# Order of TensorE products: one idle round moved from round 7 to round 2 in the opened steps of a fused Fourier filter and SiLU network

## The chip, the core and the metric

The kernel runs on one core of a Trainium2 chip. The metric is the device time of one execution in microseconds; the median over several runs is compared. The core has five engines that run their own instruction streams and wait for one another by semaphores: TensorE (PE in the profile, with its weight loads shown apart as PEld), VectorE (DVE), ScalarE (ACT), GpSimd (POOL) and SyncE (SP), which issues most of the transfers.

## What is computed

Two blocks follow each other. The first filters each of 8 sequences of 3008 tokens and 256 channels in the frequency domain; the second is a feed-forward network without a gate, with 2048 inner units.

```python
X = np.fft.rfft(x, axis=1)                  # x: (8, 3008, 256)
Y = X * (filt_r + 1j * filt_i)[None, :, :]
y = np.fft.irfft(Y, n=3008, axis=1)
h = y.reshape(24064, 256) @ w_in            # (256, 2048)
out = (h * (1.0 / (1.0 + np.exp(-h)))) @ w_out
```

All is in float32.

## The kernel before

**Tiles and steps.** The transforms are written as products with small tables of cosines and sines, in stages (`stage1`, `forward`, `inverse`, `stage3`, lines 267 to 588). Their pieces for sequence b + 1 are laid in among the work of the network for sequence b. The network takes a sequence in six pairs of token tiles: two halves, each cut into 256, 256 and 240 columns. For each pair it goes over eight blocks of the inner units. One pair with one block is a step, so there are 48 steps for a sequence (`STEPS`) and 384 in all.

**Two generators for a step.** Both products of the network use a Strassen-like scheme with seven products where eight would be needed. `hidden(step)` (line 719) makes the first layer: products named after their weight block, A11, A12, S2, S1, S3, A22 and S4. It yields between them, so that they stand in rounds 0, 1, 2, 3, 4, 6 and 7 of the step's eight rounds (round 5 has none). `project(step)` (line 778) makes the second layer for the step before, seven products that I call P1 to P7 in the order in which they are issued. Each is added up in one of four PSUM banks over the eight blocks of a pair. A product of 256 columns shows in the trace as two matmuls, each with its weight load.

**What a step waits for.** `hidden` has two PSUM banks, and only one of each. In px, A11, S2, S3 and A22 are added up one on another, and between them ScalarE copies the partial sum away (lines 740, 747 and 753) or applies the silu to it (line 736, after A22). In pyz, one half takes A12 and the other S1 and S4; VectorE combines them with the copies into g (line 703, called from `hidden`): g of round 1 after A12, g of round 4 after S3's copy, g of round 7 after S4. Px and pyz are used again by the next step: its A11 waits until the silu has read px, and its A12 until the last g has read pyz. Two subtractions that finish g of the step before (`finish`, line 767) follow g of round 1 on VectorE; P6 and P7 need them.

**What sets the order.** Every engine works in the order in which the program issues. The loop at line 1141 goes through the rounds of a step. In each round it first lets `hidden` and then `project` go on by one product, and then issues what is planned for that place: evictions, parts of the transform, stores (`put`, `pending`, `until`). In an ordinary step P1 to P7 thus stand in rounds 0 to 6.

**Opened steps.** In 20 of the steps (`opened`, filled by `open_step` at line 658) a transform piece borrows the banks px and pyz before `hidden` takes them. These are, counted within 48 steps, step 4 (six times, `stage1`), step 12 (seven times, `stage3` and `forward`) and step 38 (seven times, `stage3`). There P1 and P2 are issued ahead of the piece, to fill the time until px and pyz are free, and the other five products are held in round 0, so that they begin in round 1. With round 7 also given as held, the five stand in rounds 1 to 5. On VectorE and ScalarE an opened step has, besides the work of every step, the evictions of the piece; step 12 also has two multiplies by the filter (line 468); in step 38 the subtractions of `tokens` (line 709) and, for all sequences but the last, two operations of `fold` (line 394) for a later sequence.

The steps 52, 60 and 86 that are spoken of later are such steps 4, 12 and 38. A name with a prime, as in A11', is the product of the step after.

The loop is this:

```python
if step in opened:
    for _ in range(2):
        next(work[1])                      # P1, P2
until(step - 0.05)                         # the piece
for rnd in range(ROUNDS):
    held = work[1:] if step in opened and rnd in (0, 7) else []
    work = [w for w in work if w in held or next(w, work) is not work]
    until(step + rnd / ROUNDS)
```

Of the kernel before, what the change touches and what calls it, by code (L numbers as in the profile page):

```python
# [167 lines left out]
def kernel(  # L168
# [421 lines left out]
    joined, opened = set(), set()  # L590
# [176 lines left out]
    def finish():  # L767

        for g, n in unfinished:
            combine(v, g[:, 6, 0:n], g[:, 2, 0:n], g[:, 4, 0:n], ALU.subtract)  # L770
            combine(v, g[:, 7, 0:n], g[:, 3, 0:n], g[:, 6, 0:n], ALU.subtract)
        unfinished.clear()
# [5 lines left out]
    def project(step):  # L778

        pair, jp = divmod(step, NJP)  # L780
        n, g = pairs[pair][3], g_t.pop(step)
        if jp == 0:
            acc[pair] = {}
        last = jp == NJP - 1

        order = PROJECT
        if jp == 0 and step in joined:
            order = PROJECT[0:2] + PROJECT[3:5] + PROJECT[2:3] + PROJECT[5:]
        elif jp == 0:
            order = PROJECT[2:3] + PROJECT[0:2] + PROJECT[3:]  # L790
        for c, k, i, h in order:
            if i not in acc[pair]:
                acc[pair][i] = accps.tile([128, 2, 256], FP32, name=f"acc_{pair}_{i}", tag=f"a{i}")

            nc.tensor.matmul(out=acc[pair][i][:, h, 0:n], lhsT=w_t[:, jp, c, 1], rhs=g[:, k, 0:n],  # L795
                             start=(jp == 0 and h == 0), stop=last, skip_group_check=True)
            if last and (h == 1 or i == 3):
                drain(pair, i)
            yield
# [327 lines left out]
    for pair in range(len(pairs)):  # L1127
        step, rnd = combines[pair % per] if pair != 1 else (7, 5)
        pending.append((pair // per * STEPS + step + rnd / ROUNDS, 98, lambda pair=pair: tokens(pair)))
        for chunk in range(2 if pair < len(pairs) - 1 else 0):  # L1130
            step, rnd = stores[pair % per][chunk]
# [4 lines left out]
    def until(time):  # L1136
        while pending and pending[0][0] <= time:
            pending.pop(0)[2]()

    until(-1e-3)  # L1140
    for step in range(n_steps + LAG):
        work = []
        if step < n_steps:
            work.append(hidden(step))
        else:
            finish()
        if step >= LAG:
            work.append(project(step - LAG))
        if step in opened:
            for _ in range(2):  # L1150
                next(work[1])
        until(step - 0.05)
        for rnd in range(ROUNDS):
            held = work[1:] if step in opened and rnd in (0, 7) else []
            work = [w for w in work if w in held or next(w, work) is not work]
            until(step + rnd / ROUNDS)
        assert not work
# [30 lines left out]
```

## Time and profile before

| | before |
|---|---|
| time, median of 3 (lowest, highest) | 2591.37 us (2590.7, 2591.59) |
| span of the profiled execution | 2589.0 us |
| granted TensorE clock, mean | 0.996 |
| instructions | 48366 |
| moved to and from HBM | 96.05 MB read, 81.26 MB written |
| mean HBM traffic over the span | 68 GB/s |

The profile's page gives busy times by engine, the chain of work that ended last (followed back from the last instruction to whatever released each one) and groups of instructions by source line. The timeline gives one line to each run of equal instructions: start and duration in us, engine, line, operation, output <- inputs, and count; in square brackets the idle time of the engine before it, and what ended it. A matmul's end is modelled, so successive matmuls overlap in the timeline; the starts are the ones to go by. The table of waits gives, for each engine and line and what it waited for, the sum in us, the number of times and the longest.

### The profile page before, as it was taken

The page shows a single profiled execution, that of the slowest core. Times are in us where ns is not written, and L with a number is a line of the kernel's source. Part 1 is how long each engine was busy: PE and PEld are TensorE (multiplying, and loading weights), DVE is VectorE, ACT ScalarE, POOL GpSimd, SP SyncE. Part 2 cuts the span into 40 slices and gives each one's busy share as a digit, 9 for nine tenths or more (in the row PEclk, how much of TensorE's full clock was granted, in tenths as well). Part 3 has the DMA queues.
Part 4 walks back from the last instruction along what each step waited for, and adds up shares of the span by engine and source line. Part 5 has one row for each costly group of instructions (what it writes and reads, how often), then busy time and mean ns, then how long its engine had stood idle before and what let it go on. Part 6 is the DMA issues. An engine that isn't in the chain of part 4 may idle for free.

```text
span 2589.0 us, 48366 instructions
## 1 busy us (share of the span) xinstructions
PE 2563.1 (99%) x18972; PEld 2197.7 (85%) x18972; DVE 1681.1 (65%) x3569; ACT 1113.6 (43%) x3014; POOL 424.4 (16%) x672
## 2 busy tenths in 40 slices
PE   8999999999999999999999999999999999999998
PEld 6788888888888888888888888888888888888987
DVE  7766666666666666666666666666666676555554
ACT  3544444444444444444444444444444444444443
POOL 2211211121112111211122111211121112101101
PEclk9899999999999999999999999999999999999999
DMA  8531232222222222231223222331232211210000
GB/s 273 148 86 46 67 84 65 60 57 79 62 63 65 71 64 58 71 77 59 68 54 88 56 66 58 79 73 54 64 73 69 71 47 27 65 20 16 9 17 16
DMA packets 200077, 171.08 MB, mean 66 GB/s; under 512 B 122116, under 2 KB 174196, under 8 KB 199060
## 3 DMA queue, kind: packets, MB, share of 16 engines
q1 hardware_dynamic: 178520, 117.04, 18.9%
q0 software_dynamic: 16928, 44.65, 5.4%
q10 hardware_dynamic: 4400, 6.29, 0.8%
q8 instruction: 149, 2.44, 0.4%
q14 instruction: 80, 0.66, 0.1%
HBM read 96.05 MB, written 81.26 MB: 68 GB/s over the span
## 4 chain that ended last, share of the span: by engine, by line
PE 95%; DMA 2%; ACT 1%; DVE 1%; issue 0%; SPq 0%; ACTq 0%; DVEq 0%
PE acc L795 43%; PE px L732 26%; PE pyz L732 19%; PE pd L560 3%; PE pb L446 2%; PE pc L489 2%; PE pf L416 1%; DMA raw<-in_moe_w_in_dram 1%; DMA w_t<-in_x_dram 0%; DVE g L703 0%; PE pa L342 0%; DMA filt<-in_filt_i_dram 0%; DMA t<-d 0%; DMA e_t<-e_tbl 0%; ACT t L349 0%
## 5 line engine op out<-in xcount | busy, mean ns | idle before, releaser
L795 PE MATMUL acc<-g,w_t 128*128 128x256 f32 (+1 forms) x5376 | 1508.8, 375 | 0.4 <-DVE g L703 0.4
L795 PEld LDWEIGHTS acc<-g,w_t 128*128 128x128 f32 x5376 | 1021.3, 190 | 115.6 <-DVE g L703 0.8
L703 DVE TENSOR_TENSOR g<-pyz,abc 128x256 f32<-128x256 f32 (+1 forms) x1152 | 479.6, 416 | 617.8 <-ACT abc L753 366.5
L703 DVE TENSOR_TENSOR g<-g 128x256 f32<-128x256 f32 (+3 forms) x1152 | 599.1, 520 | 196.9 <-ACT g L736 183.7
L732 PE MATMUL px<-ty,w_t 128*128 128x256 f32 (+1 forms) x2304 | 678.1, 376 | 0.5 <-ACT abc L753 0.5
L736 ACT ACTIVATE g<-g 128x256 f32<-128x256 f32 (+1 forms) x1152 | 472.9, 410 | 242.8 <-DVE g L703 242.8
L732 PEld LDWEIGHTS px<-ty,w_t 128*128 128x128 f32 x2304 | 432.4, 190 | 64.4 <-issue 7.9
L703 POOL TENSOR_TENSOR s<-s 128x256 f32<-128x256 f32 (+1 forms) x329 | 255.0, 793 | 1414.3 <-DVE s L815 1308.9
L732 PE MATMUL pyz<-y,w_t 128*128 128x256 f32 (+1 forms) x1536 | 454.1, 377 | 0.0
L732 PEld LDWEIGHTS pyz<-y,w_t 128*128 128x128 f32 x1536 | 283.4, 189 | 47.4 <-DVE g L703 8.2
L747 ACT COPY abc<-px 128x256 f32<-128x256 f32 (+1 forms) x384 | 141.5, 368 | 367.3 <-PE px L732 367.3
L753 ACT COPY abc<-px 128x256 f32<-128x256 f32 (+1 forms) x384 | 141.9, 369 | 344.7 <-PE px L732 344.7
L736 ACT ACTIVATE g<-px 128x256 f32<-128x256 f32 (+1 forms) x384 | 146.1, 380 | 297.3 <-PE px L732 297.2
L732 PE MATMUL px<-y,w_t 128*128 128x256 f32 (+1 forms) x768 | 234.3, 387 | 2.1 <-ACT y L246 1.0
L732 PE MATMUL pyz<-ty,w_t 128*128 128x256 f32 (+1 forms) x768 | 225.6, 375 | 0.2 <-DVE g L703 0.2
L732 PEld LDWEIGHTS px<-y,w_t 128*128 128x128 f32 x768 | 138.6, 189 | 41.1 <-ACT g L736 7.7
L732 PEld LDWEIGHTS pyz<-ty,w_t 128*128 128x128 f32 x768 | 145.9, 190 | 17.5 <-DVE g L703 1.0
L740 ACT COPY abc<-px 128x256 f32<-128x256 f32 (+1 forms) x384 | 135.8, 354 | 44.6 <-PE px L732 44.6
L560 PEld LDWEIGHTS pd<-wi_t,t 48*64 48x64 f32 x4096 | 68.6, 140 | 30.2 <-ACT g L736 16.4
L560 PE MATMUL pd<-wi_t,t 48*64 48x47 f32 x4096 | 74.9, 238 | 4.9 <-DMA t<-d 2.8
L428 POOL DMA_DIRECT2D d<-tf x144 | 71.5, 503 | 31.0 <-DVE tf L424 26.9
L815 ACT COPY s<-acc 128x512 f32<-128x512 f32 (+1 forms) x94 | 54.3, 578 | 47.5 <-PE acc L795 47.4
(118 smaller groups left out, 1309.0 us busy)
## 6 DMA issues: line engine op xcount, KB each, us to landing
t<-d SPq DMA_DIRECT2D x120, 192.0 KB
d<-q POOLq DMA_DIRECT2D x86, 256.0 KB, 2.6
t<-d SPq DMA_DIRECT2D x84, 256.0 KB
out_dram<-o SPq DMA_DIRECT2D x636, 32.0 KB
d<-tf POOLq DMA_DIRECT2D x144, 96.0 KB, 3.4
xr<-in_x_dram SPq DMA_DIRECT2D x6, 1472.0 KB
x_all<-in_x_dram SPq DMA_DIRECT2D x72, 96.0 KB
x_all<-xr SPq DMA_DIRECT2D x72, 96.0 KB
```

Source lines behind the costliest of these rows:

```text
L428: nc.gpsimd.dma_start(out=d1[k // 2, :, k % 2, n0:n0 + 4], in_=us["tf"][32 * k:32 * k + NS].rearrange("p q n c -> p (q n) c"))
L446: nc.tensor.matmul(out=ps[k][32 * j:32 * j + 32, ri, :], lhsT=d_t[rows, 4 * g + at, ri, :], rhs=t2[rows, at, :], start=True, stop=True)
L489: nc.tensor.matmul(out=ps[j][64 * k:64 * k + 64, a, :], lhsT=e_t[rows, g + a, k, ri, :], rhs=zs[k][rows, ri, :], start=(a == 0 and ri == 0 ...
L560: nc.tensor.matmul(out=ps[h][c0:c0 + 64, cb, i, :], lhsT=t4s[g][rows, i, 128 * cb + c0:128 * cb + c0 + 64], rhs=wi_t[rows, :], start=True, ...
L703: eng.tensor_tensor(out=out, in0=in0, in1=in1, op=op)
L732: nc.tensor.matmul(out=out, lhsT=w_t[:, jp, c, 0], rhs=rhs, start=start, stop=True, skip_group_check=True)
L736: nc.scalar.activation(out=g[:, k, 0:n], in_=g[:, k, 0:n] if src is None else src, func=AFT.Silu)
L740: nc.scalar.copy(out=sums[:, 0, 0:n], in_=xo)
L747: nc.scalar.copy(out=sums[:, 1, 0:n], in_=xo)
L753: nc.scalar.copy(out=sums[:, 2, 0:n], in_=xo)
L795: nc.tensor.matmul(out=acc[pair][i][:, h, 0:n], lhsT=w_t[:, jp, c, 1], rhs=g[:, k, 0:n], start=(jp == 0 and h == 0), stop=last, skip_group ...
L815: copy(out=s[:, 2 * i:2 * i + 2, 0:n], in_=acc[pair][i][:, :, 0:n])
```

## The change

In opened steps the round without a product of the second layer is round 2 and no longer round 7. The five products that are left stand in rounds 1, 3, 4, 5 and 6 where they stood in rounds 1 to 5. From round 3 on an opened step then has the same order as an ordinary one. Nothing else is changed, neither an instruction nor a buffer nor a transfer.

```diff
         for rnd in range(ROUNDS):
-            held = work[1:] if step in opened and rnd in (0, 7) else []
+            held = work[1:] if step in opened and rnd in (0, 2) else []
             work = [w for w in work if w in held or next(w, work) is not work]
             until(step + rnd / ROUNDS)
```

The order on TensorE in an opened step, before and after (P3 to P7 belong to the step before):

```
before  A11 A12 P3 S2 P4 S1 P5 S3 P6 P7 A22 S4
after   A11 A12 P3 S2 S1 P4 S3 P5 P6 A22 P7 S4
```

It is for the end of the step: a product of the second layer then stands between A22, whose result ScalarE has to take out of px, and A11 of the next step, which needs px.

## The prediction

> **What bounds the kernel now.** I read the page first: engine shares, then the chain that ended last.
>
> ```profile
> PE 2563.1 (99%) x18972; PEld 2197.7 (85%) x18972; DVE 1681.1 (65%) x3569; ACT 1113.6 (43%) x3014; POOL 424.4 (16%) x672
> ...
> PE 95%; DMA 2%; ACT 1%; DVE 1%; issue 0%; SPq 0%; ACTq 0%; DVEq 0%
> ```
>
> TensorE is on the chain 95% of the span, so a change in the order of its products counts only through gaps between them. Busy shares hide such gaps. I therefore took start times from the timeline: a product of 256 columns is two matmuls, and in an undisturbed step the next starts 0.432 us later (0.405 with 240 columns). An opened step s runs P1 P2, pieces, A11 A12 P3 S2 P4 S1 P5 S3 P6 P7 A22 S4, then A11' P1' A12' P2' S2' of step s+1. Step 60, from its S2 on:
>
> ```profile
> 490.51 0.42 DVE L703 TENSOR_TENSOR g<-pyz,abc 128x256 f32<-128x256 f32 x1 [1.32 <-ACT abc L740]
> ...
> 490.67 0.59 PE L732 MATMUL px<-ty,w_t 128*128 128x256 f32 x2
> ...
> 491.30 0.37 ACT L747 COPY abc<-px 128x256 f32<-128x256 f32 x1 [0.87 <-PE px L732]
> ...
> 492.83 1.03 PE L795 MATMUL acc<-g,w_t 128*128 128x256 f32 x4
> ...
> 493.69 0.59 PE L732 MATMUL px<-ty,w_t 128*128 128x256 f32 x2
> ...
> 494.12 0.59 PE L732 MATMUL pyz<-y,w_t 128*128 128x256 f32 x2
> 494.32 0.39 ACT L736 ACTIVATE g<-px 128x256 f32<-128x256 f32 x1 [0.92 <-PE px L732]
> ...
> 494.76 0.30 PEld L732 LDWEIGHTS px<-y,w_t 128*128 128x128 f32 x2 [0.45 <-ACT g L736]
> 494.76 0.70 PE L732 MATMUL px<-y,w_t 128*128 128x256 f32 x2
> ...
> 495.30 0.59 PE L795 MATMUL acc<-g,w_t 128*128 128x256 f32 x2
> ```
>
> The reader is to see that P6 and P7 (492.83, x4) stand before A22 (493.69), and that only S4 (494.12) stands between A22 and A11' (494.76). A11' overwrites the px bank that the silu at 494.32 still reads; its weight load starts 0.05 us after that silu ends. S4 to P1' takes 1.173 us in the trace's nanoseconds instead of 0.863: 0.31 us lost. The table of waits for the load queue has this wait with nearly the count of the opened steps (20), and the wait of the next part:
>
> ```profile
> PEld pyz L732 <- DVE g L703: 9.2, 37, 0.6
> ...
> PEld px L732 <- ACT g L736: 7.9, 21, 0.4
> ```
>
> I added the excess over 0.432 (0.405) from P3 to S2' for all 20 opened steps. They fall in two classes: steps 4 and 12 of each 48 (six and seven steps; "early") lose 0.304 to 0.306 us each, all at A11'. Step 38 of each 48 (seven; "late") loses 0.398 to 0.406, the last one (326) 0.305. Together 6.68 us. The late steps look different (step 86):
>
> ```profile
> 663.75 0.41 DVE L703 TENSOR_TENSOR g<-pyz,abc 128x256 f32<-128x256 f32 x1
> 664.07 1.28 DVE L407 TENSOR_TENSOR uf<-x_all 120x512 f32<-120x512 f32 x2
> 664.21 0.30 PEld L732 LDWEIGHTS pyz<-y,w_t 128*128 128x128 f32 x2 [0.30 <-DVE g L703]
> ...
> 664.78 0.30 PEld L732 LDWEIGHTS px<-y,w_t 128*128 128x128 f32 x2 [0.28 <-ACT g L736]
> ...
> 665.27 0.42 DVE L703 TENSOR_TENSOR g<-pyz,abc 128x256 f32<-128x256 f32 x1
> ...
> 665.74 0.30 PEld L732 LDWEIGHTS pyz<-y,w_t 128*128 128x128 f32 x2 [0.23 <-DVE g L703]
> ```
>
> Here VectorE works without a pause from 660.52 to 665.69: g of round 1, two finishing subtractions, three of tokens (ty), the y copy, g of round 4 (663.75), two folds (664.07), g of round 7 (665.27). S4 waits for the second g, A11' for the silu, A12' for the last g.
>
> **What the skill says.** "TensorE: Matmul & The Clock Gate", section "Step-by-step: what each phase is for": matmuls stay in program order while weight loads are pulled ahead of them. The trace agrees: an undisturbed load starts 0.216 us before its matmul. Section "LDWEIGHTS (loading the stationary operand)" prices a load at columns / 1.2, so 107 ns for 128. The trace bears it out: a load that starts x after the matmul ahead of it costs nothing up to about 0.11, then x - 0.11 (x = 0.100: nothing; 0.125: 0.017; 0.205: 0.095; 0.280: 0.169; 0.420: 0.309). "PSUM — Partial Sum Buffer", section "PSUM bank collisions raise a hardware error", says that two engines may not be in the same bank and quadrant at once. So S1, which writes one half of pyz, has to wait for the g that reads the other half. In the ordinary steps no S1 load starts less than 52 ns after that g ends, which agrees. "Perfetto Trace Analysis", section "Tensor Engine Instruction (MATMUL, LD_WEIGHTS)", says that ends on TensorE are estimates; I use starts alone.
>
> **The change, part by part.** Nothing is added or removed. In the 20 opened steps P4 to P7 move one round later, so the order becomes A11 A12 P3 S2 S1 P4 S3 P5 P6 A22 P7 S4. On TensorE S1, S3 and A22 start 0.432 us earlier, S4 and what follows keep their place. VectorE and ScalarE keep their order. P4 to P7 only get more time for their inputs, and nothing waits for them within the step: cost nothing, hidden by the products put ahead.
>
> S1 (early, step 60): the load would start at 490.89. The g of round 1 ends at 490.93 and releases it at 490.98, x = 0.100 after the matmul at 490.88, just inside the 0.11. Cost 0; bounds 0 and 0.10 (a restart as A11' shows). In late steps x = 0.088.
> S3 now has two products behind S2 instead of three: load due at S2 + 1.079 = 491.75; the copy (491.30 + 0.37) releases it at 491.73. Cost 0, with 0.025 to spare, as S2's own place and its copy don't move.
> A22: the copy of S3 starts 0.632 after S3 (491.96 + 0.63 = 492.60), ends 492.97, releases at 493.02; the load is due at 493.04. Cost 0. In steps 4 a t copy stands before it on ScalarE, to 438.57 + 0.59 = 439.16; the copy behind it is due at 439.28, so it is not held.
> S4, early: g of round 4 comes 0.43 earlier with S3, cost 0.
> A11', early: the silu follows A22 by 0.632, so 493.89 to 494.27, releases at 494.32; with P7 between, the load is due at 494.34. The whole 0.305 goes.
> A12', early: behind S4 it waits for the last g: S4 + 0.632 + 0.424 + 0.052 = S4 + 1.108. Its load is due at S4 + 1.079, x = 0.03: free, and this is where the ordinary steps stand (1.11). In step 60 the two multiplies by the filter that stand before this g on VectorE follow the earlier g and so end 0.43 earlier; they no longer hold it. Queued behind that g on VectorE is the double subtraction, then g of the next step; its next S1 load is due 0.19 later than that g permits. Cost 0.
> Late: the second g ends at 664.16 by VectorE's own queue, whatever S3 does. S4 is still due at 664.14, its load is 0.28 late: 0.169 lost as now (now 0.063 at S4 and the rest at A11'). A11' is then free. But the last g stays at 665.27 to 665.69, held by the folds, and releases A12' at 665.74, where it is released now. P2' then starts at 665.74 + 0.320 + 0.216 = 666.28, against 666.27 now. Gain 0. Step 326 has no fold: A12' is free, S4's 0.169 stays, gain 0.305 - 0.169 = 0.14.
> Sum: 13 x 0.305 + 0.14 = 4.1 us, so 2591.37 - 4.1 = 2587.3. The shift lasts: after early steps VectorE next idles on a copy from ScalarE that TensorE sets (0.47 us before g at the end of step 61), so it follows.
>
> **Rivals.** (a) Late steps gain too, if the folds don't really hold the last g, or the A12' wait isn't on it: 6.68 us all told, 2584.7. For: A12' shows only 0.094 of the loss now. Against: its load starts 0.05 after that g in every late step but the last. (b) The gain is given back: S1 or S3, with 0.01 and 0.025 us to spare, waits anew, or VectorE holds the step after as in the late ones; no change, 2591.4. For: the thin margins. Against: a miss of 0.02 costs 0.02. (c) Slower: S1 and S3 both pay a full wait as A11' does, 2 x 0.309. Then the early steps lose 0.618 - 0.305 = 0.313 and the late 0.618: 13 x 0.313 + 7 x 0.618 = 8.4, 2599.8. For: S1 is put nearer to a bank that is being read. Against: waits in the trace start from a known end + 0.05, which gives neither.
>
> **How the numbers follow.** The sum above 0.70, (a) 0.12, (b) 0.12, (c) 0.06. Faster by over 0.2% (below 2586.2) is (a) and a small tail of the first: 0.17. Slower is (c): 0.06. Within: 0.77. The range 2584.5 to 2590.0 holds the first and (a), and part of the cases between the first and (b); full (b) and (c) are left out, under 0.2.
>
> **What would show it.** After the change the wait of px loads on the silu's g falls from 21 to about one; in step 60 S4 to P1' is 0.863; S1 loads start 0.05 after g without a longer S1. In step 86 the A12' wait grows from 0.23 to about 0.36 and the A11' wait goes. I am wrong if S1, S3 or A22 shows a matmul of 0.70 in place of 0.59, if A12' in late steps comes at its turn, or if new waits appear in steps 5, 13 or 39.

## The result, and the profile after

| | before | after |
|---|---|---|
| median of 22 runs each (lowest, highest) | 2590.67 us (2588.51, 2594.33) | 2586.22 us (2584.17, 2589.04) |
| ratio after / before, 95% interval | | 0.9982 [0.9976, 0.9989] |
| excess over the product rhythm, P3 to S2', 20 opened steps | 6.68 us | 2.52 us |
| the same, all steps | 21.46 us | 17.33 us |

The change takes 4.45 us off by the medians. A second set of runs of the same kernel (e10 below) gave 2586.12 against 2590.07, 3.95 us and ratio 0.9984 [0.9976, 0.9991]. The sum over the trace scatters far less (the trace of e10 gives 17.36 for the same kernel) and says 21.46 - 17.33 = 4.13 us. For that sum each product is compared with the 0.432 us (0.405 with 240 columns) to the next one in an undisturbed step, and what it takes more is added up. Places where a transform piece stands between two products can't be compared in this way. The whole stretch from A11 of step 1 to the last product of the kernel has them too: it took 2489.69 us before, 2486.03 after and 2485.86 in e10, so 3.66 and 3.84 us less.

One thing about the change itself. Before, the five held products of an opened step had run out with round 5, so rounds 6 and 7 were both without one, and the 7 in the program held nothing back. What the change does to the order is to leave round 2 without a product and to give P7 to round 6, the round of A22; round 7 has none before or after.

On the page nothing but TensorE's busy time seems to move. These are the engine shares and the chain that ended last, after:

```profile
PE 2560.6 (99%) x18972; PEld 2198.1 (85%) x18972; DVE 1681.0 (65%) x3569; ACT 1113.9 (43%) x3014; POOL 424.9 (16%) x672
...
PE 95%; DVE 2%; DMA 1%; ACT 1%; issue 0%; ACTq 0%; SPq 0%; DVEq 0%
```

TensorE did the same 18972 matmuls with 2.5 us less of "busy". Most of a stall counts as busy: between A12 and S2' of the 20 opened steps busy time falls by 3.61 us and idle time only from 0.55 us to nothing. (The total falls by less, as the start of the kernel, up to A11 of step 1, has 1.1 us more of it in this trace.) The timeline shows where the stalls were. Step 60 after the change, from g of round 1 on (start, duration, engine, line, operation, output <- inputs):

```profile
490.88 0.42 DVE L703 TENSOR_TENSOR g<-pyz,abc 128x256 f32<-128x256 f32 x1 [1.31 <-ACT abc L740]
491.05 0.59 PE L732 MATMUL px<-ty,w_t 128*128 128x256 f32 x2
...
491.36 0.31 PEld L732 LDWEIGHTS pyz<-ty,w_t 128*128 128x128 f32 x2
491.48 0.59 PE L732 MATMUL pyz<-ty,w_t 128*128 128x256 f32 x2
...
493.63 0.59 PE L732 MATMUL px<-ty,w_t 128*128 128x256 f32 x2
...
494.07 0.59 PE L795 MATMUL acc<-g,w_t 128*128 128x256 f32 x2
494.27 0.38 ACT L736 ACTIVATE g<-px 128x256 f32<-128x256 f32 x1 [0.92 <-PE px L732]
...
494.50 0.59 PE L732 MATMUL pyz<-y,w_t 128*128 128x256 f32 x2
...
494.72 0.41 PEld L732 LDWEIGHTS px<-y,w_t 128*128 128x128 f32 x2
494.93 0.59 PE L732 MATMUL px<-y,w_t 128*128 128x256 f32 x2
...
495.36 0.59 PE L795 MATMUL acc<-g,w_t 128*128 128x256 f32 x2
```

A22 (493.63), P7 (494.07), S4 (494.50), A11' (494.93) and P1' (495.36) now follow one another at 0.43 us, and the load for A11' at 494.72 carries no wait: the silu that it needs ended at 494.65. S4 to P1' takes 0.864 us in the trace's nanoseconds where it took 1.173. The table of waits of the load queue has no row any more for px loads behind the silu's g (21 waits, 7.9 us before). The row for pyz loads behind VectorE's g is still there:

```profile
PEld pyz L732 <- DVE g L703: 9.7, 34, 0.6
```

Part of it comes from the late steps. Step 86:

```profile
663.79 0.41 DVE L703 TENSOR_TENSOR g<-pyz,abc 128x256 f32<-128x256 f32 x1
...
664.12 1.28 DVE L407 TENSOR_TENSOR uf<-x_all 120x512 f32<-120x512 f32 x2
...
664.25 0.30 PEld L732 LDWEIGHTS pyz<-y,w_t 128*128 128x128 f32 x2 [0.29 <-DVE g L703]
...
664.57 0.41 PEld L732 LDWEIGHTS px<-y,w_t 128*128 128x128 f32 x2
...
665.32 0.41 DVE L703 TENSOR_TENSOR g<-pyz,abc 128x256 f32<-128x256 f32 x1
...
665.78 0.30 PEld L732 LDWEIGHTS pyz<-y,w_t 128*128 128x128 f32 x2 [0.37 <-DVE g L703]
```

The wait of the px load (664.57) has gone here too. But VectorE's last g still starts right behind the folds, 1.53 us after the second g (1.52 before), and the load for A12' waits 0.37 us for it where it waited 0.23. The step loses 0.39 us as against 0.40.

All 20 opened steps fall into these two kinds, early and late. The 13 early steps went from 0.304 to 0.306 us of loss each to none. Six late steps lose 0.39 to 0.41 as before, and step 326, which has no fold, went from 0.305 to 0.165.

### The profile page after: what moved, and what is told of

It is laid out like the page before. It is cut to its first block, busy times and chain, and to the rows that moved or that the text cites. A ratio compares the mean times of both kernels' runs of the same rounds, so it can differ in the third digit from the quotient of the medians.

```text
span 2586.3 us, 48366 instructions
## 1 busy us (share of the span) xinstructions
PE 2560.6 (99%) x18972; PEld 2198.1 (85%) x18972; DVE 1681.0 (65%) x3569; ACT 1113.9 (43%) x3014; POOL 424.9 (16%) x672
## 4 chain that ended last, share of the span: by engine, by line
PE 95%; DVE 2%; DMA 1%; ACT 1%; issue 0%; ACTq 0%; SPq 0%; DVEq 0%
PE acc L795 43%; PE px L732 25%; PE pyz L732 19%; PE pd L560 3%; PE pb L446 2%; PE pc L489 2%; PE pf L416 1%; DMA w_t<-in_x_dram 0%; DVE g L703 0%; PE pa L342 0%; DMA filt<-in_filt_r_dram 0%; DMA d_t<-d_tbl 0%; PE pa L333 0%; DMA raw<-in_moe_w_out_dram 0%; ACT t L349 0%
```

## The experiments

My theory: the early steps give the gain because P7 covers the time in which the silu reads px; the late steps give none because VectorE's queue sets their end. The rivals: (a) every opened step gains about alike; (d) the gain comes from a general shift of the later work; (e) A12' of the late steps waits on something else than VectorE's queue; and, for the order, a reading by which any order with P7 behind A22 would do. In each diff the line with + is the experiment.

**One part alone: e1, early steps; e2, late steps.**

```diff
-            held = work[1:] if step in opened and rnd in (0, 7) else []
+            idle = (0, 7) if step % STEPS == 38 else (0, 2)     # e1; e2 has the two exchanged
+            held = work[1:] if step in opened and rnd in idle else []
```

> The new order in steps 4 and 12 of each 48 alone (13 steps), the old order in step 38. My theory: all but 0.14 us of the gain comes from these 13 steps, 0.31 us each, so about 4.0 us less than before (ratio 0.9985), and the loss between P3 and S2' of the next step is zero in the early steps and stays at 0.40 us in the late ones. Rival a (every opened step gains about alike): 13/20 of the 4.45 us, 2.9 us less (0.9989). Rival d (the gain is not from these steps but from a general shift of the later work): less than 2 us.

> The new order in step 38 of each 48 alone (7 steps). My theory: VectorE holds the end of these steps wherever the products stand, so six of them lose 0.40 us as before and the last one 0.17 instead of 0.31: 0.1 us less than before, ratio 1.0000 within what can be measured. Rival a: 7/20 of the gain, 1.6 us less (0.9994), and the loss between P3 and S2' falls below 0.3 us in each.

| | median | before beside it | ratio, 95% interval | loss in opened steps, sum |
|---|---|---|---|---|
| e1, early alone | 2586.31 us | 2590.33 us | 0.9984 [0.9976, 0.9991] | 2.65 us |
| e2, late alone | 2589.43 us | 2590.33 us | 0.9997 [0.9989, 1.0006] | 6.53 us |

e1 takes 4.0 us off by the medians and 4.03 by the loss (6.68 - 2.65); its late steps lose 0.39 to 0.41 as before, but for step 326 with 0.30. Rival (d), with less than 2 us, falls. e2's sum falls by 0.14 us, all of it in step 326; its medians differ by 0.9 us, within its interval, which holds no change as well as rival (a)'s 0.9994. The sum over the trace decides: rival (a) wanted less than 0.3 us in each late step, and six of them lose 0.39 to 0.41.

**Where the idle round stands: e3 round 1, e4 round 4, e5 round 3.**

```diff
-            held = work[1:] if step in opened and rnd in (0, 2) else []
+            held = work[1:] if step in opened and rnd in (0, 1) else []     # e3; e4: (0, 4); e5: (0, 3)
```

> The idle round is round 1 instead of 2: A11 A12 S2 P3 S1 P4 S3 P5 P6 A22 P7 S4. A product still stands between A22 and S4, so a theory by which only that place counts expects the time of after. Mine: S2 needs the copy of A11's sum out of px, and now has only A12 ahead of it; the copy releases it 0.41 (steps 4) or 0.46 us (steps 12) after the matmul ahead, less 0.11: 0.30 and 0.35 us lost at S2 in each early step, nothing at A11' of the next step, late steps 0.40 in all as before. Sum over the 20 steps 7.0 us (before 6.7, after 2.5), so about the time of before.

> The idle round is round 4: A11 A12 P3 S2 P4 S1 P5 S3 P6 A22 P7 S4. P7 again stands behind A22. Mine: A22 has only P6 between itself and S3, whose copy releases it 0.41 us after the matmul ahead, so 0.30 us is lost at A22 in each early step and none at A11' of the next; late steps 0.40 in all. Sum over the 20 steps 6.6 us (before 6.7, after 2.5), about the time of before. A theory by which only the place behind A22 counts expects the time of after.

> The idle round is round 3: A11 A12 P3 S2 P4 S1 S3 P5 P6 A22 P7 S4. S3, A22 and S4 stand as in after; only S1 and P4 change places. The S1 load then comes 0.43 us later and is clear of the g that reads the other half of pyz. My theory: S1's wait costs nothing in after (0.100 us late against 0.11), so this gives the time of after within 0.1 us in sum over the opened steps (2.5 us lost). If S1's wait did cost something in after that the starts don't show, this is faster than after.

Step 60 of e3, load queue, S2 in the second line; then of e4, from S3's copy on, with A22 in the last two:

```profile
489.13 0.41 PEld L732 LDWEIGHTS pyz<-y,w_t 128*128 128x128 f32 x2
490.02 0.30 PEld L732 LDWEIGHTS px<-ty,w_t 128*128 128x128 f32 x2 [0.49 <-ACT abc L740]
```

```profile
491.86 0.37 ACT L753 COPY abc<-px 128x256 f32<-128x256 f32 x1 [1.04 <-PE px L732]
...
492.28 0.30 PEld L732 LDWEIGHTS px<-ty,w_t 128*128 128x128 f32 x2 [0.43 <-ACT abc L753]
492.28 0.70 PE L732 MATMUL px<-ty,w_t 128*128 128x256 f32 x2
```

| | one run | loss from A12 to S2', 20 steps | lost in an early step, and where |
|---|---|---|---|
| before | | 6.67 us | 0.31 at A11' |
| e3, round 1 | 2590.65 us | 6.94 us | 0.297 (steps 4) and 0.352 (steps 12), at S2 |
| after, round 2 | | 2.51 us | none |
| e5, round 3 | 2586.18 us | 2.53 us | none |
| e4, round 4 | 2589.46 us | 6.47 us | 0.297 at A22 |

Step 60 of e5, the load for S1, without a wait:

```profile
490.26 0.41 PEld L732 LDWEIGHTS pyz<-ty,w_t 128*128 128x128 f32 x2
```

In all three P7 stands behind A22 and A11' does not wait, yet by their sums e3 and e4 gain nothing (each of the three ran once, and single runs scatter too much to decide): the copy that empties px then has one product of cover at another place. The wait moved rather than went, at the size that the lateness less 0.11 us gives: the load starts 0.407 us (S2, steps 4), 0.462 us (S2, steps 12) and 0.408 us (A22) after the start of the matmul ahead. Of the orders run, rounds 2 and 3 are those in which each reader of px has two products of cover. From A11 to A11' an opened step has eight products that don't write px, for four readers, so two each is the only share that leaves none with less. The six late steps with folds lose 0.39 to 0.41 us in e3, e4 and e5 too, wherever the first of their waits falls. e5 also settles the thinnest margin of the prediction: there S1 comes a product later, clear of g's read in the other half of pyz, and nothing is gained by it. So S1's load, which in after starts 0.086 to 0.102 us after the matmul ahead, costs nothing.

**What holds the late steps: e6, folds; e7 and e9, tokens; e8, tokens without the change.**

```diff
-            for f, step, load, places in ((0, -56, -66, ((-60, 3), (-60, 5), (-59, 5), (-58, 5))),
+            for f, step, load, places in ((0, -56, -66, ((-60, 3), (-60, 5), (-59, 5), (-57, 5))),     # e6, from after
```

```diff
-    combines = ((-2, 1), (6, 1), (11, 5), (22, 5), (26, 6), (38, 1))
+    combines = ((-2, 1), (6, 1), (11, 5), (22, 5), (26, 6), (34, 1))     # e7 from after, e8 from before; e9 from after: (39, 1)
```

> After, with the last two fold operations moved from step 38 round 5 to step 39 round 5 for the first fold of each sequence. My theory: the folds hold the last g of step 38; without them A12' of step 39 doesn't wait, and only S4's wait for the second g is left: 0.17 us in each of the seven late steps in place of 0.40 in six of them; sum over the 20 steps 1.1 us instead of 2.5. Rival e (A12' waits on something else than VectorE's queue): 0.40 stays. The folds may cost something in step 39; step 37 carries as many without a wait.

> After, with the tokens of the pair that begins in step 40 made in step 34 instead of step 38 (1.5 us of VectorE). My theory: VectorE's queue is then free before the second g of step 38, so neither S4 nor A12' waits and the late steps lose nothing either: sum over the 20 opened steps about 0 instead of 2.5, 2.5 us less than after and 6.6 less than before (ratio 0.9974). Rival e: late steps keep 0.40, the time of after. Rival f: step 34 has no room and gives the 2.5 us back.

> Before, with the same move of the tokens. My theory: the late steps then look like the early ones before the change, 0.305 us each at A11', instead of 0.40: 0.6 us less than before (ratio 0.9998). So the move alone is worth 0.6 us, the change alone 4.1, both 6.6: each of the two waits of the late steps hides the other. If the two are independent, the move is worth 2.5 here as well (0.9990).

| | time | ratio to before, 95% interval | loss in opened steps | loss in all steps |
|---|---|---|---|---|
| after | 2586.22 us | 0.9982 [0.9976, 0.9989] | 2.52 us | 17.33 us |
| e6, folds in step 39 | 2583.39 us (one run) | | 1.11 us | 15.93 us |
| e7, tokens in step 34 | 2587.42 us | 0.9993 [0.9984, 1.0001] | -0.09 us | 18.84 us |
| e8, the same without the change | 2593.57 us | 1.0014 [1.0007, 1.0021] | 6.10 us | 25.03 us |

The before that ran beside e6, e7 and e8 has a median of 2589.82 us, 0.85 us under the one beside after; the times of the first row and of the others are not to be subtracted, the losses are. A loss of -0.09 us is none: the rhythm is rounded up to 0.432 us.

e6: with the folds gone the last g of step 86 waits for S4 and no longer for VectorE, and A12' no longer waits for it; what stays is S4's own wait, 0.161 to 0.173 us a step.

```profile
661.32 0.30 PEld L732 LDWEIGHTS pyz<-y,w_t 128*128 128x128 f32 x2 [0.30 <-DVE g L703]
...
662.06 0.42 DVE L703 TENSOR_TENSOR g<-pyz,abc 128x256 f32<-128x256 f32 x1 [0.79 <-PE pyz L732]
...
662.54 0.38 PEld L732 LDWEIGHTS pyz<-y,w_t 128*128 128x128 f32 x2
```

e7: the late steps lose nothing, as I expected, and rival (e) falls. But my expectation of the time was wrong, and rival (f) of its expectation came true: seven of the eight steps 34 now lose 0.58 us each, 4.1 in all, more than the 2.6 won. In step 82 (a step 34) two subtractions that take the inverse transform out of PSUM (line 533) are queued behind the tokens, g of round 4 behind them, and S4 waits:

```profile
633.17 0.65 DVE L703 TENSOR_TENSOR ty<-y 128x480 f32<-128x480 f32 x1
633.86 0.85 DVE L703 TENSOR_TENSOR ty<-y,ty 128x240 f32<-128x240 f32 x2
634.63 1.40 DVE L533 TENSOR_TENSOR q<-q,pc 128x512 f32<-128x512 f32 x2
...
635.95 0.42 DVE L703 TENSOR_TENSOR g<-pyz,abc 128x256 f32<-128x256 f32 x1
...
636.42 0.30 PEld L732 LDWEIGHTS pyz<-y,w_t 128*128 128x128 f32 x2 [0.72 <-DVE g L703]
```

In the profile of after VectorE is busy for 4.10 us of the 6.04 us of a step 34, so 1.5 us more fits by the sum; it doesn't fit ahead of g. I had looked at the steps' operations, not at their place. e8's time was forecast wrong in the same way: not 0.6 us less than before but slower, by the same 4.1 us in steps 34. Its opened steps still answer the question it was made for. Without the change the move takes 0.58 us off them (6.68 to 6.10), and the late ones lose 0.305 us each, all at A11', as here in step 86:

```profile
666.75 0.30 PEld L732 LDWEIGHTS px<-y,w_t 128*128 128x128 f32 x2 [0.44 <-ACT g L736]
```

The change takes 4.16 off, both together 6.77. The two waits of a late step, that on the silu and that on VectorE's queue, hide each other: to take away either alone brings 0.1 us or nothing, both bring 0.40.

**A version that is faster than both: e9, beside after once more, e10.**

> After, with the tokens of the pair that begins in step 40 made in step 39 instead of step 38. In the trace of after step 39 has 2.8 us of work for VectorE in 6.3, step 38 has 5.3 in 5.5. My theory: the late steps lose nothing, as with the tokens in step 34, and step 39 takes 1.5 us more without a wait (ordinary steps with tokens do): sum over the 20 opened steps about 0 instead of 2.5, no new loss elsewhere, 2.6 us less than after and 6.7 less than before (ratio 0.9974). Rival f: step 39 too gives it back, as step 34 did: the time of after (0.9983).

> After once more, beside the run with the tokens in step 39: 4.1 us less than before by the sum of the trace, ratio 0.9984, and about 2.6 us more than the run beside it.

| | median | before beside it | ratio, 95% interval | loss in opened steps | loss in all steps |
|---|---|---|---|---|---|
| e9, tokens in step 39 | 2583.56 us | 2590.07 us | 0.9973 [0.9963, 0.9984] | -0.09 us | 14.74 us |
| e10, after | 2586.12 us | 2590.07 us | 0.9984 [0.9976, 0.9991] | 2.53 us | 17.36 us |

Step 39 takes the tokens without a wait. VectorE in step 86 and 87 of e9:

```profile
661.61 1.28 DVE L407 TENSOR_TENSOR uf<-x_all 120x512 f32<-120x512 f32 x2
...
663.02 0.42 DVE L703 TENSOR_TENSOR g<-pyz,abc 128x256 f32<-128x256 f32 x1
...
663.50 0.38 PEld L732 LDWEIGHTS pyz<-y,w_t 128*128 128x128 f32 x2
```

```profile
665.67 0.65 DVE L703 TENSOR_TENSOR ty<-y 128x480 f32<-128x480 f32 x1
666.35 0.85 DVE L703 TENSOR_TENSOR ty<-y,ty 128x240 f32<-128x240 f32 x2
667.31 0.42 DVE L703 TENSOR_TENSOR g<-pyz,abc 128x256 f32<-128x256 f32 x1
```

The folds end 0.13 us before the last g starts, and A12' (663.50) carries no wait; in step 87 the tokens end at 667.20 and the next g starts at 667.31. 2.56 us are won over e10 by the medians and 2.62 by the sum over the trace. The two intervals overlap a little; the sum, which scatters by hundredths, decides.

## Why the prediction was right

It said 2587.3 from a time before of 2591.37, a fall of 4.1 us; the trace's sum fell by 4.13 and the medians by 4.45 and 3.95. The measured 2586.22 lies within the range. That the difference of the medians came so near the sum is in part chance, and so is the place of the absolute time: the base of 2591.37 was the median of 3 runs, that of all 22 is 2590.67, and from that the same sum gives 2586.6. What bears the mechanism out is the trace. Point by point:

- **The early steps.** Forecast 13 x 0.305; measured 0.309 to 0.310 each (from 0.305 to -0.005; the last 5 ns come from a rhythm rounded to 0.432). e1 shows that they alone carry it, all but the 0.14 us of step 326.
- **S1 at no cost.** Forecast 0.100 us late against 0.11: measured 0.100 to 0.102 in the early steps, no longer matmul, and e5 shows no gain where it is taken away.
- **S3, A22, A11' and A12' at no cost.** All four loads start at their turn or inside the tolerance. Of the four, A12' starts 0.03 late, as forecast. e3 and e4 show what one product less of cover costs at S2 and A22, so the second product is needed there. For S3 no run has only one.
- **The late steps.** Forecast no gain in six, P2' at the same place, the A12' wait up from 0.23 to 0.36 us and S4's kept: measured 0.37 and 0.29 (0.30). The gain in step 326 was put at 0.14: 0.140. That the folds hold the last g was argued then, from operations that follow one another without a pause; e6 shows it, and e9 shows that the tokens hold both g.
- **The shift lasts.** Steps 5 and 13 show no new wait, step 39 only the one of A12' that was forecast; the rest of the kernel loses the same as before (21.46 - 6.68 = 14.78 against 17.33 - 2.52 = 14.81). Apart from the opened steps and those right behind them no step's loss differs by more than 0.025 us between the two traces.
- **What I had wrong on the side.** The late steps could have been had as well. I put (a) at 0.12 as something that the change might do by itself, and didn't see that it needs one more constant, the place of the tokens.

The trace's gain lies 0.3 us under the first medians' and 0.2 over the second's; the runs of one kernel lie 3 to 6 us apart, so nothing more can be read from that.

## What to carry to other kernels

When an engine is 99% busy, look for gaps in the start times of its instructions against the rhythm of an undisturbed stretch, and measure each gap in products of cover: here a reader of px on ScalarE needs two products between the writer and the next writer, at each of the three places where a run had only one (about 0.3 us lost each time), and a filler taken from one place opens the gap at another unless that place had three. A step whose two waits come from two engines can show next to no gain when either is mended (here 0.1 us or nothing of 0.40); find the second wait before the first change is judged. Before work is moved to an engine's emptier step, look at what is queued behind it there, not only at the sum.

## What I had not expected

A step with 1.9 us of free VectorE time lost 0.58 us to 1.5 us of added work (step 34 in e7), because the work was ahead of an operation that TensorE waits for, while step 39 took the same work for nothing. And the rule for a late weight load was sharper than I thought it would be: the losses that it gave for e3, e4 and after before they ran (0.30 and 0.35 at S2, 0.30 at A22, 0 at S1) came out as 0.297, 0.352, 0.297 and 0.
